# Remainder channels of attention scores and dP: four key chunks at four row positions of TensorE

## The chip, the cores and the metric

The kernel runs on one core of one Trainium2 chip. The metric is the device time of one execution in microseconds; the median of the kernel before is 1481.88 us over three runs (1480.46 to 1482.83).

## The reference

The reference is the forward pass and all gradients of one layer of a Branchformer, for x of shape (2, 4000, 144) in bf16. Only the attention branch bears on this change:

```
xa = layernorm(x)
q, k, v = split(xa @ w_qkv)              # D = 144 each
p = softmax((q @ k.T) * D ** -0.5)       # 4000 x 4000 for each of the two sequences
glob = (p @ v) @ w_att_out
... a local branch (gelu, layernorm, depthwise convolution of 5 taps), merged with glob by
    another convolution of 5 taps and w_merge, added to x
returns out and the gradients of x and of all seven weights
```

There is one head, 144 channels wide. Since 144 = 128 + 16, every product that contracts over channels is split into a part of 128 channels and a remainder of 16.

## The kernel before, in words

The two sequences are worked through one after the other. For each, the 4000 tokens lie as 32 blocks of 125 (NB = 32, PB = 125). The weights are folded ahead of time, so that scores are `Q xa^T` with Q = xa M1 (M1 = scaled w_q w_k^T), and the gradient of the probabilities is `dP = G xa^T` with G the gradient that reaches the attention through the merge convolution, folded with w_v and w_att_out. Both products take the same right-hand side: xa, transposed. It is kept as `xaT_m` (128 channels by 4000 tokens) and, for the other 16 channels, in rows 0 to 15 of `R` (128 by 4000; rows 16 to 111 hold the remainder channels of grad_out, rows 112 to 127 zeros). `pre_pieces` makes these, in four groups of eight blocks: `xat(g)` transposes on TensorE and copies the 16 remainder rows into R on VectorE (L346).

`phase_att` is the stage that the change touches. One step t of its loop (L812) does the following for query block i = t and for the blocks before it, as a software pipeline:

- `jit_mm(t+1)` computes Q and G of the next block into `qb` (two parts of 256 columns, of which 144 are channels and the rest zeros); `jit_tr(t+1)` transposes this into `qt`, four tiles of 128 rows by 125 columns: Q's 128 channels, Q's remainder (16 rows and 112 rows of zeros), and the same two of G.
- `S_pair(t, c2)`, four times: a PSUM tile from the pool `ps_sg` (two tiles of two banks each) takes two key chunks of 500 (CH) tokens. Each chunk is a matmul over 128 channels (L679) and one over the remainder (L680) with all 128 rows of `qt` and `R`, the zeros of `qt` masking the rows of R that don't belong. VectorE then finds the running minimum of the negated scores (L684, L686, one operation of 1000 columns), and ScalarE writes exp(score + that) into `Pbuf` (L687).
- `rescale(t)` brings the first three pairs to the last one's maximum (L692, L696, L698) and starts a DMA transpose of the block's Pbuf into `PT` on SyncE's queue (L699).
- `Y_half(t-1, h)`, two halves: 32 matmuls of PT with xa (L707), and then the row sums' reciprocal, delta, and the scaled copies (L713 to L721).
- `dP_pair(t-1, c2)`, four times: as S_pair with G (L729, L730), and then VectorE writes dS = (dP - delta) * P into `Sbuf`, one operation for each chunk of 500 (L735).
- `Z_half(t-2, h)`: 32 matmuls of the transposed dS (`ST`, by a DMA transpose, L855) with xa (L751); `zt_tr(t-3)` transposes the result.
- `X_group`: dx's share, sixteen blocks in six groups of up to three, each with two or more pairs of matmuls (L790) into a tile of the pool `ps_w` (three banks), added into `acc` by VectorE (L796).
- `local(upto)`: the next few of some 280 small pieces of the local branch, spread over the steps.

PSUM's eight banks are thus taken: four by ps_sg, three by ps_w (X, jit_mm, jit_tr, zt_tr and the local branch), one by Y and Z. An inner loop over s = 0 to 7 (L822) fixes the order: s below 4 has a pair of scores, s from 4 on a pair of dP, and the rest stands between them. The framework orders each engine's queue by this sequence, but lets an instruction that is ready sooner by its own estimate go ahead, except where an edge forbids it. Each engine then works strictly through its queue.

## Time and profile before

The profiled execution took 1482.13 us, its span from the first to the last instruction 1480.4 us, at a mean granted TensorE clock of 0.984.

| stretch of the span, us | what runs there |
|---|---|
| 0 to 52 | loads, layernorm, weights, transposes of the first sequence |
| 52 to 643 | attention and local branch, first sequence (32 steps; the first L684 at 62.0, the last at 638.9) |
| 643 to 772 | merge and gradients, first sequence; preparation of the second |
| 772 to 1358 | attention and local branch, second sequence (L684 from 775.1 to 1351.2) |
| 1358 to 1480 | merge, gradients, weights' gradients |

| group of instructions | count | busy us | mean ns |
|---|---|---|---|
| L679, scores, 128 channels, PE | 512 | 194.1 | 379 |
| L680, scores, remainder, PE | 512 | 193.5 | 378 |
| L729, dP, 128 channels, PE | 512 | 192.8 | 377 |
| L730, dP, remainder, PE | 512 | 191.4 | 374 |
| L735, dS, VectorE | 512 | 355.8 | 731 |
| L687, exponentials, ScalarE | 256 | | 1097 (median) |

How to read it: PE is TensorE's matmuls, PEld its weight loads, DVE VectorE, ACT ScalarE, POOL GpSimd, SP SyncE. The duration of a matmul includes the way through the array, so matmuls one behind the other overlap in the records: their cost in a full queue is the distance from one start to the next, which is less than the mean duration.

### The profile page before, as it was taken

How to read it: one execution, taken by the hardware profiler on the slowest of the kernel's cores; microseconds unless marked ns; L12 is line 12 of the kernel's file. 1: busy time of each engine (PE TensorE's matmuls, PEld its weight loads, DVE VectorE, ACT ScalarE, POOL GpSimd, SP SyncE). 2: the span in 40 equal slices, each digit the busy share in tenths (PEclk: the TensorE clock that was granted, in tenths of full speed). 3: DMA queues.
4: the chain of work that ended last, by engine and by line, in shares of the span. 5: the costliest groups of instructions: out<-in, count | busy, mean ns of one | idle time of the engine just before them, and what ended most of it. 6: DMA issues, size and time to landing. Idle time of an engine off the chain costs nothing. (4 is left out here: it accounts for less than half of the span.)

```text
span 1480.4 us, 39159 instructions
## 1 busy us (share of the span) xinstructions
PE 1387.0 (94%) x16184; PEld 1191.1 (80%) x16184; DVE 1218.0 (82%) x3061; ACT 851.2 (57%) x1538; POOL 282.1 (19%) x493
## 2 busy tenths in 40 slices
PE   2789999999999999997888999999999999999898
PEld 1568888888888888887875888888888888888797
DVE  6689898988898988887638998889898889888754
ACT  1666666666566655632637666666666656554182
POOL 8210111110111110027521112120101010101420
PEclk9899999999999999998999999999999999999999
DMA  3176666666665665577215765667666666666812
GB/s 103 27 145 122 121 121 121 111 126 113 117 116 113 121 121 103 115 136 209 64 54 106 138 122 113 111 118 126 116 123 121 121 120 121 119 115 123 214 35 64
DMA packets 559360, 170.44 MB, mean 115 GB/s; under 512 B 542443, under 2 KB 554093, under 8 KB 559136
## 3 DMA queue, kind: packets, MB, share of 16 engines
q1 hardware_dynamic: 553338, 155.43, 55.6%
q0 software_dynamic: 4768, 12.14, 3.2%
q8 instruction: 126, 2.06, 0.6%
q10 hardware_dynamic: 1076, 0.38, 0.1%
q14 instruction: 52, 0.43, 0.1%
HBM read 21.07 MB, written 14.16 MB: 24 GB/s over the span
## 5 line engine op out<-in xcount | busy, mean ns | idle before, releaser
L735 DVE SCALAR_TENSOR_TENSOR Sbuf<-ps,delta,Pbuf 125x500 bf16<-125x500 f32 x512 | 355.8, 731 | 29.5 <-PE ps L730 26.8
L790 PE MATMUL X<-QBs,Sbuf 125*125 125x144 bf16 x2048 | 302.7, 226 | 6.0 <-DVE acc L796 2.6
L790 PE MATMUL X<-QBs,Pbuf 125*125 125x144 bf16 x2048 | 301.9, 226 | 0.0
L790 PEld LDWEIGHTS <-Pbuf 125*125 125x125 bf16 x2048 | 261.7, 137 | 14.3 <-issue 9.8
L790 PEld LDWEIGHTS <-Sbuf 125*125 125x125 bf16 x2048 | 261.8, 136 | 7.7 <-DVE Sbuf L735 2.0
L796 DVE TENSOR_TENSOR acc<-X,acc 125x432 f32<-125x432 f32 x372 | 203.2, 549 | 32.7 <-PE X L790 31.7
L679 PE MATMUL ps<-xaT_m,qt 128*125 128x500 bf16 x512 | 194.1, 379 | 10.7 <-ACT Pbuf L687 9.5
L729 PE MATMUL ps<-xaT_m,qt 128*125 128x500 bf16 x512 | 192.8, 377 | 6.1 <-ACT Pbuf L687 4.6
L680 PE MATMUL ps<-R,qt 128*125 128x500 bf16 x512 | 193.5, 378 | 0.0
L730 PE MATMUL ps<-R,qt 128*125 128x500 bf16 x512 | 191.4, 374 | 0.0
L707 PEld LDWEIGHTS <-PT 125*125 125x125 bf16 x2048 | 153.5, 138 | 24.2 <-DMA PT<-Pbuf 6.4
L751 PEld LDWEIGHTS <-ST 125*125 125x125 bf16 x1984 | 147.1, 137 | 18.1 <-DMA ST<-Sbuf 0.6
L707 PE MATMUL yz<-xa_aug,PT 125*125 125x145 bf16 x2048 | 157.2, 229 | 3.7 <-DMA PT<-Pbuf 3.6
L751 PE MATMUL yz<-xa_aug,ST 125*125 125x144 bf16 x1984 | 151.0, 227 | 0.4 <-DMA ST<-Sbuf 0.4
L680 PEld LDWEIGHTS <-qt 128*125 128x125 bf16 x512 | 70.3, 137 | 32.6 <-issue 13.3
L543 POOL TENSOR_TENSOR A_dwc<-l_fl,A_dwc 128x512 f32<-128x512 f32 (+2 forms) x48 | 35.9, 748 | 293.8 <-ACT l_fl L542 293.8
L730 PEld LDWEIGHTS <-qt 128*125 128x125 bf16 x512 | 69.5, 136 | 26.1 <-issue 6.7
L684 DVE TENSOR_SCALAR_CACHE_REDUCE Pbuf<-ps 125x1000 bf16<-125x1000 f32 x64 | 76.6, 1197 | 14.6 <-PE ps L680 14.4
L729 PEld LDWEIGHTS <-qt 128*125 128x125 bf16 x512 | 70.0, 137 | 22.5 <-DVE Sbuf L735 2.0
L679 PEld LDWEIGHTS <-qt 128*125 128x125 bf16 x512 | 70.3, 137 | 21.8 <-ACT qt L663 1.2
L755 ACT ACTIVATE zn<-yz,rl 125x144 bf16<-125x144 f32 x64 | 24.3, 379 | 109.7 <-PE yz L751 109.7
L413 POOL TENSOR_SCALAR l_a<-l_sq 125x576 bf16<-125x576 bf16 x32 | 21.5, 672 | 294.5 <-ACT l_sq L411 254.2
(806 smaller groups left out, 3058.6 us busy)
## 6 DMA issues: line engine op xcount, KB each, us to landing
Yn_d<-yn SPq DMA_DIRECT2D x64, 35.2 KB
Zn_d<-zn SPq DMA_DIRECT2D x64, 35.2 KB
ug_d<-ugr SPq DMA_DIRECT2D x32, 70.3 KB
xo<-in_x_dram SPq DMA_DIRECT2D x16, 140.6 KB
out_dram<-dxo SPq DMA_DIRECT2D x16, 140.6 KB
go_h<-in_grad_out_dram POOLq DMA_DIRECT2D x4, 504.0 KB, 7.0
Zn<-Zn_d SPq DMA_DIRECT2D x4, 504.0 KB
PT<-Pbuf SPq DMA_TRANSPOSE x64
```

The lines of the kernel that those rows point to most:

```text
L543: nc.gpsimd.tensor_tensor(acc, fl[0:rows, 0:n], acc, op=ALU.add)
L679: nc.tensor.matmul(ps[:, h, 0:CH], qt[:, 0, :], xaTm[:, cs], start=True, stop=False)
L680: nc.tensor.matmul(ps[:, h, 0:CH], qt[:, 1, :], R[:, cs], start=False, stop=True)
L684: nc.vector.tensor_scalar(pdst, src, -1.0, None, op0=ALU.mult, op1=ALU.min, accum_out=nm[:, 0:1])
L707: nc.tensor.matmul(Y, PT[0:PB, j, 0:PB], xaa[:, j, :], start=(j == 0), stop=(j == NB - 1))
L729: nc.tensor.matmul(ps[:, h, 0:CH], qt[:, 2, :], xaTm[:, cs], start=True, stop=False)
L730: nc.tensor.matmul(ps[:, h, 0:CH], qt[:, 3, :], R[:, cs], start=False, stop=True)
L735: nc.vector.scalar_tensor_tensor(sdst, ps[:, h, 0:CH].rearrange("p (a b) -> p a b", b=PB), DL[i][:], psrc, op0=ALU.subtract, op1=ALU.mult)
L751: nc.tensor.matmul(Z, ST[0:PB, j, 0:PB], xaa[:, j, 0:D], start=(j == 0), stop=(j == NB - 1))
L755: nc.scalar.activation(zn[:, 0:D], Z, ACT.Copy, scale=RL.pop(i)[:])
L790: nc.tensor.matmul(X[:, jj, :], l, r, start=(n_ == 0), stop=(n_ == len(ops) - 1))
L796: nc.vector.tensor_tensor(av, X[:, 0:nj, :], av, op=ALU.add)
```

## The change

Four things are changed, the first three of them together.

1. The 16 remainder channels of xa are laid out a second time, in a new tile `XR` (128 by 2 by 500): key chunk c stands in rows 32 (c mod 4) to 32 (c mod 4) + 15, at place c // 4. Two DMAs on SyncE's queue for each xat(g) copy them there from R. On the other side, GpSimd repeats the 16 remainder columns of qb at columns 32, 64 and 96 of the same 128, so that after jit_tr the remainder tiles of qt hold the 16 rows four times, at rows 0, 32, 64 and 96.
2. `S_pair` and `dP_pair` become `S_quad` and `dP_quad`, two of each a step. A quad takes both tiles of ps_sg, issues the four matmuls over 128 channels, and behind the last of them (an edge, `issue_after`, holds the order) the four remainder matmuls, each with 16 rows at its own row position and into its own PSUM bank.
3. The order of a step is written out anew: scores 0; zt_tr, X, local; jit_mm, X, local; scores 1; both halves of Y; rescale; local, X, local; dP 0; jit_tr, X, local, X; dP 1; both halves of Z; X, local; what is left of X.
4. dS is computed with one VectorE operation of 1000 columns for two chunks, in place of one for each.

```diff
@@ -344,6 +344,9 @@
             for bi in range(8):
                 nc.tensor.transpose(pr[0:DR, bi, 0:PB], S.xa_aug[:, 8 * g + bi, 128:D], W.ident[0:PB, 0:PB])
             nc.vector.tensor_copy(v8(S.R, 8 * g, 8)[0:DR], pr[0:DR, :, 0:PB])
+            for c in (2 * g, 2 * g + 1):
+                r = 32 * (c % 4)
+                nc.sync.dma_start(S.XR[r:r + DR, c // 4, :], S.R[0:DR, c * CH:(c + 1) * CH])
 
         def go_rem():
             nc.gpsimd.tensor_copy(S.go_r[:], go_q[:, :, 128:D])
@@ -637,7 +640,7 @@
             nc.gpsimd.memset(t_[:, :, D:256], 0.0)
         for t_ in znr:
             nc.gpsimd.memset(t_[:, D:256], 0.0)
-        xaTm, R, xaa = S.xaT_m, S.R, S.xa_aug
+        xaTm, R, XR, xaa = S.xaT_m, S.R, S.XR, S.xa_aug
         QT, QB, RL, DL, YZ, ZN, ZT, NM, DHT = {}, {}, {}, {}, {}, {}, {}, {}, {}
         units = local_units(k, W, b, S, A, es_loc, DHT, ps_w)
 
@@ -651,6 +654,8 @@
                 nc.tensor.matmul(pj[:, D:2 * D], S.goT[:, h * PB:(h + 1) * PB], W.VUT[:, kk, 0:D], start=False, stop=(kk == 4))
             qb = qbr[i % 3]
             nc.scalar.copy(qb[:, :, 0:D], pj[:].rearrange("p (a b) -> p a b", b=D))
+            rem_ = qb[:, :, 128:256].rearrange("p a (r c) -> p a r c", c=32)[:, :, :, 0:DR]
+            nc.gpsimd.tensor_copy(rem_[:, :, 1:4, :], rem_[:, :, 0:1, :].to_broadcast([PB, 2, 3, DR]))
             QB[i] = qb
 
         def jit_tr(i):
@@ -666,25 +671,35 @@
         def pchunk(pb, c2):
             return Pbuf[0:PB, pb, c2 * 1024:(c2 + 1) * 1024]
 
-        def S_pair(i, c2):
-            qt = QT[i]
-            if c2 == 0:
+        def quad(qt, q, m):
+
+
+            pp = [ps_sg.tile([PB, 2, 512], F32, tag="sg", name="ps") for _ in range(2)]
+            for r in range(4):
+                c = 4 * m + r
+                mm = nc.tensor.matmul(pp[r // 2][:, r % 2, 0:CH], qt[:, q, :], xaTm[:, c * CH:(c + 1) * CH], start=True, stop=False)
+            with tc.issue_after(mm.ins):
+                for r in range(4):
+                    rs = slice(32 * r, 32 * r + DR)
+                    nc.tensor.matmul(pp[r // 2][:, r % 2, 0:CH], qt[rs, q + 1, :], XR[rs, m, :], start=False, stop=True)
+            return pp
+
+        def v2(ap):
+            return ap.rearrange("p h (a b) -> p h a b", b=PB)
+
+        def S_quad(i, m):
+            if m == 0:
                 nm_ = small.tile([PB, 8], F32, tag="nm")
                 NM[i] = nm_
             nm = NM[i]
-            ps = ps_sg.tile([PB, 2, 512], F32, tag="sg")
-            for h in range(2):
-                c = 2 * c2 + h
-                cs = slice(c * CH, (c + 1) * CH)
-                nc.tensor.matmul(ps[:, h, 0:CH], qt[:, 0, :], xaTm[:, cs], start=True, stop=False)
-                nc.tensor.matmul(ps[:, h, 0:CH], qt[:, 1, :], R[:, cs], start=False, stop=True)
-            src = ps[:, :, 0:CH].rearrange("p h (a b) -> p h a b", b=PB)
-            pdst = pchunk(i % NPB, c2).rearrange("p (h a b) -> p h a b", h=2, b=128)[:, :, :, 0:PB]
-            if c2 == 0:
-                nc.vector.tensor_scalar(pdst, src, -1.0, None, op0=ALU.mult, op1=ALU.min, accum_out=nm[:, 0:1])
-            else:
-                nc.vector.tensor_scalar(pdst, src, -1.0, nm[:, c2 - 1:c2], op0=ALU.mult, op1=ALU.min, accum_out=nm[:, c2:c2 + 1])
-            nc.scalar.activation(pdst, src, ACT.Exp, bias=nm[:, c2:c2 + 1], scale=1.0)
+            for c2, ps in enumerate(quad(QT[i], 0, m), 2 * m):
+                src = v2(ps[:, :, 0:CH])
+                pdst = pchunk(i % NPB, c2).rearrange("p (h a b) -> p h a b", h=2, b=128)[:, :, :, 0:PB]
+                if c2 == 0:
+                    nc.vector.tensor_scalar(pdst, src, -1.0, None, op0=ALU.mult, op1=ALU.min, accum_out=nm[:, 0:1])
+                else:
+                    nc.vector.tensor_scalar(pdst, src, -1.0, nm[:, c2 - 1:c2], op0=ALU.mult, op1=ALU.min, accum_out=nm[:, c2:c2 + 1])
+                nc.scalar.activation(pdst, src, ACT.Exp, bias=nm[:, c2:c2 + 1], scale=1.0)
 
         def rescale(i):
             nm = NM.pop(i)
@@ -720,19 +735,11 @@
             nc.sync.dma_start(S.Yn_d[:, i, :], yn[:])
             nc.scalar.activation(QBs[:, i % NPB], qb[:, :, 0:D], ACT.Copy, scale=rl[:])
 
-        def dP_pair(i, c2):
-            qt = QT[i]
-            ps = ps_sg.tile([PB, 2, 512], F32, tag="sg")
-            for h in range(2):
-                c = 2 * c2 + h
-                cs = slice(c * CH, (c + 1) * CH)
-                nc.tensor.matmul(ps[:, h, 0:CH], qt[:, 2, :], xaTm[:, cs], start=True, stop=False)
-                nc.tensor.matmul(ps[:, h, 0:CH], qt[:, 3, :], R[:, cs], start=False, stop=True)
-            for h in range(2):
-                c = 2 * c2 + h
-                psrc = Pbuf[0:PB, i % NPB, c * 512:(c + 1) * 512].rearrange("p (a b) -> p a b", b=128)[:, :, 0:PB]
-                sdst = Sbuf[0:PB, i % NDB, c * 512:(c + 1) * 512].rearrange("p (a b) -> p a b", b=128)[:, :, 0:PB]
-                nc.vector.scalar_tensor_tensor(sdst, ps[:, h, 0:CH].rearrange("p (a b) -> p a b", b=PB), DL[i][:], psrc, op0=ALU.subtract, op1=ALU.mult)
+        def dP_quad(i, m):
+            for c2, ps in enumerate(quad(QT[i], 2, m), 2 * m):
+                psrc = pchunk(i % NPB, c2).rearrange("p (h a b) -> p h a b", h=2, b=128)[:, :, :, 0:PB]
+                sdst = Sbuf[0:PB, i % NDB, c2 * 1024:(c2 + 1) * 1024].rearrange("p (h a b) -> p h a b", h=2, b=128)[:, :, :, 0:PB]
+                nc.vector.scalar_tensor_tensor(sdst, v2(ps[:, :, 0:CH]), DL[i][:], psrc, op0=ALU.subtract, op1=ALU.mult)
 
         def last_tr(c2):
 
@@ -819,37 +826,44 @@
                 for _ in range(n):
                     if xg:
                         X_group(*xg.pop(0))
-            for s in range(8):
-                if s < 4 and ok(t):
-                    S_pair(t, s)
-                if s >= 4 and ok(t - 1):
-                    dP_pair(t - 1, s - 4)
-                if t == NB and s == 4:
-                    M.late_y()
-                if s == 0:
-                    if ok(t - 3):
-                        zt_tr(t - 3)
-                    x(1)
-                elif s == 1:
-                    if ok(t + 1):
-                        jit_mm(t + 1)
-                    x(1)
-                elif s in (2, 3):
-                    if ok(t - 1):
-                        Y_half(t - 1, s - 2)
-                    if s == 3 and ok(t):
-                        rescale(t)
-                elif s == 4:
-                    if ok(t + 1):
-                        jit_tr(t + 1)
-                    x(1)
-                elif s == 5:
-                    x(1)
-                else:
-                    if ok(t - 2) and t < NB:
-                        Z_half(t - 2, s - 6)
-                    x(1)
-                local(-(-n_units * (8 * t + s + 1) // (8 * (NB - 1))))
+            def loc(f):
+                local(-(-int(n_units * (t + f) * 1000) // (1000 * (NB - 1))))
+            if ok(t):
+                S_quad(t, 0)
+            if ok(t - 3):
+                zt_tr(t - 3)
+            x(1)
+            loc(0.2)
+            if ok(t + 1):
+                jit_mm(t + 1)
+            x(1)
+            loc(0.4)
+            if ok(t):
+                S_quad(t, 1)
+            for h in range(2):
+                if ok(t - 1):
+                    Y_half(t - 1, h)
+            if ok(t):
+                rescale(t)
+            loc(0.5)
+            x(1)
+            loc(0.6)
+            if ok(t - 1):
+                dP_quad(t - 1, 0)
+            if t == NB:
+                M.late_y()
+            if ok(t + 1):
+                jit_tr(t + 1)
+            x(1)
+            loc(0.85)
+            x(1)
+            if ok(t - 1):
+                dP_quad(t - 1, 1)
+            for h in range(2):
+                if ok(t - 2) and t < NB:
+                    Z_half(t - 2, h)
+            x(1)
+            loc(1.0)
             x(6)
             if t < NB and ok(t - 1):
                 nc.sync.dma_start_transpose(out=ST[:], in_=Sbuf[:, (t - 1) % NDB, :])
@@ -1287,6 +1301,7 @@
     bx = pool(ctx, "bx", "left")
     xaT_m = bx.tile([128, T], BF, name="xaT_m")
     R = bx.tile([128, T], BF, name="R")
+    XR = bx.tile([128, 2, CH], BF, name="XR")
     go_r = bx.tile([PB, NB + 6, DR], BF, name="go_r")
     goT = bx.tile([128, (NB + 4) * PB], BF, name="goT")
     acc = bx.tile([PB, NB, D], F32, name="acc")
@@ -1296,7 +1311,7 @@
     SS = [K() for _ in range(B)]
     SS[0].xa_aug = px0.tile([PB, NB, D + 1], BF, name="xa_aug0")
     for b, S in enumerate(SS):
-        S.xaT_m, S.R, S.go_r, S.goT, S.acc, S.rstd_x = xaT_m, R, go_r, goT, acc, rstd[b]
+        S.xaT_m, S.R, S.XR, S.go_r, S.goT, S.acc, S.rstd_x = xaT_m, R, XR, go_r, goT, acc, rstd[b]
         for nm in ("Yn", "ug", "Zn"):
             setattr(S, nm + "_d", tc.dram_tile([PB, NB, D], BF, name="%s_d%d" % (nm, b)))
     A = K()
```

## The prediction

> **What bounds the kernel now.** I read the page first, then busy time by window, then the waits inside the attention stage, then single instructions in order of time.
>
> The page's busy line and the two attention stages (one for each of the two sequences) as windows:
>
> ```profile
> PE 1387.0 (94%) x16184; PEld 1191.1 (80%) x16184; DVE 1218.0 (82%) x3061; ACT 851.2 (57%) x1538; POOL 282.1 (19%) x493
> ```
>
> ```profile
> 74.00:643.00 569.00, 557.61 (x6361) 475.34 (x6361) 501.82 (x1163) 353.09 (x632) 69.01 (x109) 0.99 0.65 120
> 783.00:1358.00 575.00, 561.20 (x6394) 477.36 (x6394) 507.30 (x1174) 359.35 (x642) 81.34 (x136) 1.00 0.66 121
> ```
>
> The columns are window, its length, busy PE, PEld, DVE, ACT, POOL, granted clock, DMA share, GB/s. These stages hold 1144 of the 1480.4 us, and in them PE is busy 1118.8 us (98%), DVE 1009.1 (88%). The granted clock is 1.00. A busy PE alone proves little, so the waits in 111 to 629 us come next (us in total, times, longest):
>
> ```profile
> PE ps L729 <- ACT Pbuf L687: 1.3, 2, 0.8
> ```
>
> ```profile
> DVE Pbuf L686 <- PE ps L680: 23.8, 34, 1.9
> DVE Sbuf L735 <- PE ps L730: 12.2, 20, 1.5
> ```
>
> All waits of PE that this view lists add up to under 8 us in 518; DVE's to about 56, nearly all for PE. So PE's queue sets the pace, and an instruction less on it is worth its issue time as long as DVE can follow. The first scores reduction of a step (L684) comes every 18.9 us in the steady steps (mean of 28 intervals in the timeline); start to start, PE's instructions fill 18.6 us of that and DVE's 16.8.
>
> The prices are start-to-start distances. Timeline of PE, one pair of score groups, and of DVE:
>
> ```profile
> 316.00 0.38 PE L679 MATMUL ps<-xaT_m,qt 128*125 128x500 bf16 x1
> 316.21 0.37 PE L680 MATMUL ps<-R,qt 128*125 128x500 bf16 x1
> 316.42 0.37 PE L679 MATMUL ps<-xaT_m,qt 128*125 128x500 bf16 x1
> 316.63 0.37 PE L680 MATMUL ps<-R,qt 128*125 128x500 bf16 x1
> 316.84 1.22 PE L707 MATMUL yz<-xa_aug,PT 125*125 125x145 bf16 x16
> ```
>
> ```profile
> 306.15 1.38 DVE L735 SCALAR_TENSOR_TENSOR Sbuf<-ps,delta,Pbuf 125x500 bf16<-125x500 f32 x2
> ...
> 315.50 1.25 DVE L686 TENSOR_SCALAR_CACHE_REDUCE Pbuf<-ps,nm__4761 125x1000 bf16<-125x1000 f32 x1
> 316.68 0.08 DVE L686 DVE_READ_ACCUMULATOR Pbuf<-ps,nm__4761 125x1 f32 x1
> ```
>
> A matmul of 500 columns costs 0.21 us of PE whether its 128 rows hold 128 channels (L679) or 16 (L680). Two L735 of 500 columns take 1.38, one 0.73, so the second adds 0.65; one operation of 1000 columns (L686) lets the next start after 1.18.
>
> **The change, part by part.**
>
> **Remainder matmuls.** L680 and L730 are 512 each, 1024 in all, or 256 groups of four. Removed per group: 4 x 0.21 = 0.84 us. Added per group: four matmuls of 16 rows at four row positions, and two passages, from full-height to 16-row matmuls and back. No row has four matmuls at different row positions, so their time is bounded: 0.21 if they run at once, 0.84 if in turn. Between: each needs its own weight load, and X's pairs of load and matmul (L790) start every 0.063 us, so loads one behind the other put the fourth matmul 3 x 0.063 = 0.19 after the first, and the group takes 0.19 + 0.21 = 0.40. I take 0.40, because that is the nearest row on loads. The passage has a row: full-height and 16-row transposes in turn, in the preparation of the weights.
>
> ```profile
> 42.47 0.26 PE L231 MATMUL pt<-ident,Wi 128*96 128x128 bf16 x1
> 42.65 0.20 PE L232 MATMUL pt<-ident,Wi 16*96 16x16 bf16 x1
> 42.79 0.26 PE L231 MATMUL pt<-ident,Wi 128*96 128x128 bf16 x1
> 42.97 0.20 PE L232 MATMUL pt<-ident,Wi 16*96 16x16 bf16 x1
> ```
>
> A pair takes 42.79 - 42.47 = 0.32 us. Eight transposes of one height (L341 at 48.85) take 0.60 with the last one's 0.22, so they start 0.055 apart and two would take 0.11; the passage there and back costs 0.32 - 0.11 = 0.21. So a group costs 0.40 + 0.21 = 0.61 in place of 0.84: 0.23 saved, 256 x 0.23 = **-59 us**. Bounds: 0.21 + 0.21 gives -108 us, 0.84 + 0.21 gives +54 us.
>
> The Trainium skill, "TensorE: Matmul & The Clock Gate", section Part 3 (Packing small matmuls), gives a speedup of 3.07 for four 32-row tiles at 512 columns; no run here shows it yet. By it the group would take 0.84 / 3.07 = 0.27 (an estimate from that page), the saving be 0.36 a group or 92 us, and the sum below come to about 1409 us.
>
> **PSUM hand-over.** The pool for scores and dP has two tiles of two chunks. Before, a pair takes one tile and PE can be one pair ahead. Now a group of four chunks takes both, and its third main matmul waits until the group before has been read out of the second tile. From the last issue of a group: 0.21 until DVE starts (316.84 to 317.05), then for scores two reductions of 1.2 and the exponential of the second (L687, 1.1, starting 0.1 later): 3.8. For dP: 0.21 + 2 x 1.18 + 0.06 until PE follows (L735's end to L729 at 303.68) = 2.6. PE's own work in the meantime, from the same timeline (X group of 12: 0.75; Y or Z: 2.1; jit_mm 0.50; jit_tr 0.22; zt_tr 0.11; the local units 2.4 a step in the new shares), with 0.42 for the two main matmuls in the first tile:
> - scores 0 to scores 1: 0.11 + 1.50 + 0.50 + 0.96 + 0.42 = 3.5 against 3.8: 0.3 short
> - scores 1 to dP 0: 2.1 + 0.75 + 0.48 + 0.42 = 3.75 against 3.8: even
> - dP 0 to dP 1: 0.22 + 1.50 + 0.60 + 0.42 = 2.7 against 2.6: covered
> - dP 1 to the next step: 2.1 + 0.75 + 0.36 + 0.42 = 3.6 against 2.6: covered
>
> That is 0.3 a step if DVE takes each group at once: 64 x 0.3 = **+19 us**. It doesn't always do so now: in the timeline of steps 2 to 29, L684/L686 start 0.23 us later than the 0.04 behind their matmul that is the least, L735 0.66 later. With these on top the first two and the third hand-over are short by 0.53, 0.26 and 0.52: 1.3 a step, +84 us. Below 19 it goes to 0 if X or local matmuls stand in the gap. I take 19, since DVE gets free time in this change and catches up whenever PE waits.
>
> **dS in operations of 1000 columns.** Four pairs a step at 1.18 in place of 0.73 + 0.65 - 0.08 = 1.30: 0.12 x 4 = 0.5 us a step, 31 us of DVE over 64 steps. DVE isn't the bound, so **0** in the sum. It takes DVE to 16.3 of a step. If nothing were saved there, 16.8 would still lie below PE's new 17.7 (18.6 - 4 x 0.23).
>
> **The rest.** The POOL copy that repeats the 16 channels three times: nearest rows are L455 (125x64, 0.24) and L433 (125x288, 0.42), so some 0.35, 64 times, on an engine busy 59.7 of 518 us. It lies between the copy of qb (ends 314.56) and the transposes of qb (318.78): 4.2 us of slack, so 0; without cover 22 us. Behind it on POOL stand the local units' copies and sums, which it delays by 0.35. The sixteen copies into XR go on SP's queue: the nearest issue is L460 (0.65), and landings of POOL's DMAs lie between 2.1 and 10.3 us. The last copy of R ends at 50.7 and 763.5, the first score matmul starts at 59.9 and about 772, so they have 9 us: 0, at most 2 us. SP waits there for L346; behind it stand stores of finished output (L1052, every 4.6 us), which nothing waits for. The order of Y, Z, X and local units is new, their count is not: 0. X's sums (L796) now find DVE taken for 2.4 us by a group in place of 1.2; three buffers cover that (PE waited 1.3 us in 518 for them), taken as 0, and up to 1.2 us a step or 77 us if the cover is gone.
>
> **Sum.** 1482.13 us is the profiled execution (span 1480.4; the median of three is 1481.88): 1482.1 - 59 + 19 = **1442 us**, and the 0.25 us between the two don't move it.
>
> **The rivals.**
> 1. *The hand-over eats the gain.* At each group PE stands at the third main matmul because DVE, in its own order, is still at sums and local work. For it: at most pairs DVE now starts late (by 0.66 at dP). Against: DVE waited 56 us for PE in 518, so the lateness is PE's order, not want of DVE time. It decides from 0.92 us of waits a step (4 x 0.23); at today's lateness it is 1.3: 1482 - 59 + 84 = **1507 us**, slower. The Trainium skill, "TensorEngine Tiling (Array Packing)", section PSUM Bottleneck, warns of the same: tiling speeds up TensorE, not the reading out of PSUM.
> 2. *The four don't overlap*, and the change doesn't do what it says: 1482 + 54 + 19 = **1555 us**. For it: nothing in this trace ever overlaps two matmuls. Against: nothing either; only the rows' heights allow it.
> 3. *They run wholly at once*, loads hidden: 1482 - 108 + 19 = **1393 us**. For it: weight loads in this trace lie under matmuls that run. Against: after a passage, L232's load starts only 0.15 us after L231 began, so the first load isn't hidden. The skill's 3.07 above lies between this and my forecast.
> 4. *Waits and saving cancel*: 1470 to 1494.
>
> **How the numbers follow.** Forecast (1415 to 1470) 0.40; rival 1 0.25; rival 2 0.07; rival 3 0.20; rival 4 0.08, of which 0.03 within 0.2% (about what a measurement here can tell from no change), 0.02 faster, 0.03 slower. Faster 0.40 + 0.20 + 0.02 = 0.62, same 0.03, slower 0.25 + 0.07 + 0.03 = 0.35. The range runs from just below rival 3 to past rival 1 with part of X's 77 us: 1385 to 1530; it leaves out rival 2 and the tails.
>
> **What would show it.** The four remainder matmuls of a group should start some 0.06 apart (near 0: rival 3; 0.21: rival 2); the next full-height matmul should start 0.6 after the fourth main one ended its issue. PE's waits for Pbuf (L687's successor) and Sbuf in a steady stage should rise from 2 to about 8 us; 25 or more is rival 1. dS should show 256 operations near 1.25 us. The step should go from 18.9 to 18.3. The prediction fails if the four start 0.21 apart, or if PE's idle time a step passes 0.9 us.

## The result and the profile after

The changed kernel takes 1535.17 us (median; 1532.82 to 1537.37) against 1481.17 (1477.91 to 1482.83) for the kernel before on the same chip: a ratio of 1.0359, interval 1.0345 to 1.0374. It is 54 us slower. The forecast was 1442 us, the range 1385 to 1530; the time lies past the range, on the side of rival 1.

The lines have moved: main matmuls L680, remainders L684 (scores and dP alike), reductions L699 and L701, exponentials L702, rescale L711, Y L722, dS L742, X L797, sums L803. First the busy line of the page, then three windows: the two attention stages and the steady stretch 111 to 629 us (window, length, busy PE, PEld, DVE, ACT, POOL, granted clock, DMA share, GB/s).

```profile
PE 1339.5 (87%) x16184; PEld 1086.5 (71%) x16184; DVE 1193.8 (78%) x2805; ACT 851.0 (55%) x1538; POOL 301.8 (20%) x557
```

```profile
74.00:660.00 586.00, 533.72 (x6351) 425.23 (x6351) 489.28 (x1040) 351.93 (x629) 76.27 (x134) 0.99 0.55 116
800.00:1406.00 606.00, 541.72 (x6410) 430.70 (x6410) 497.71 (x1058) 359.93 (x639) 89.90 (x164) 0.98 0.63 115
111.00:629.00 518.00, 473.60 (x5703) 379.26 (x5701) 433.72 (x924) 315.99 (x567) 68.04 (x119) 1.00 0.54 114
```

PE is busy 1075 of 1192 us in the two stages (90%, before 98%), and no other engine has come up: DVE falls to 83%, ACT stays near 60%. No engine is full now. Where the time went is in the waits of 111 to 629 us (total us, times, longest) and in the chain that ended last (share of the span by engine):

```profile
PE ps L680 <- ACT Pbuf L702: 22.9, 44, 1.3
...
DVE Pbuf L701 <- PE ps L684: 13.3, 16, 1.6
DVE Pbuf L699 <- PE ps L684: 11.4, 13, 1.8
...
PE ps L680 <- DVE Sbuf L742: 8.6, 21, 0.9
```

```profile
DVE 35%; PE 33%; ACT 15%; DMA 6%; issue 6%; POOL 5%; DVEq 0%; POOLq 0%; SPq 0%; ACTq 0%
```

PE's main matmuls wait 31.5 us for the readers of their PSUM tiles, where this stretch showed 1.8 us of such waits before, and under 8 us of PE's waits in all. At the same time DVE still waits 24.7 us for PE's scores (29.9 before). Each waits for the other: DVE has 35, PE 33 and ACT 15% of the chain.

The groups (line, engine, operation, out and in, count; busy us, mean ns of one; idle time ahead and what ended most of it):

```profile
L680 PE MATMUL ps<-xaT_m,qt 128*125 128x500 bf16 x1024 | 298.4, 381 | 97.8 <-ACT Pbuf L702 64.9
L742 DVE SCALAR_TENSOR_TENSOR Sbuf<-ps,delta,Pbuf 125x1000 bf16<-125x1000 f32 x256 | 311.0, 1253 | 16.4 <-PE ps L684 16.3
...
L684 PE MATMUL ps<-XR,qt 16*125 16x500 bf16 x1024 | 112.9, 428 | 0.0
...
L684 PEld LDWEIGHTS <-qt 16*125 16x125 bf16 x1024 | 35.9, 129 | 98.4 <-issue 98.4
```

The remainders do overlap: 1024 of 428 ns would be 438 us one behind the other, and the union is 112.9, a quarter. Their weight loads overlap as well: 1024 x 129 ns = 132, the union 35.9. One hand-over, from the second scores group of a step to the first of dP, on three engines, as timelines of PE, DVE and ACT (start, duration, engine, line, operation; in brackets the idle time before it and what ended it):

```profile
306.32 0.43 PE L684 MATMUL ps<-XR,qt 16*125 16x500 bf16 x4
...
309.88 0.58 PE L680 MATMUL ps<-xaT_m,qt 128*125 128x500 bf16 x2
311.44 0.58 PE L680 MATMUL ps<-xaT_m,qt 128*125 128x500 bf16 x2 [0.97 <-ACT Pbuf L702]
311.95 0.43 PE L684 MATMUL ps<-XR,qt 16*125 16x500 bf16 x4
312.31 0.39 PE L666 MATMUL pt<-ident,qb 125*128 125x125 bf16 x4
```

```profile
306.95 0.46 DVE L419 TENSOR_TENSOR l_z<-l_a,l_hs 125x576 bf16<-125x576 bf16 x1 [0.34 <-POOL l_a L416]
307.33 1.25 DVE L701 TENSOR_SCALAR_CACHE_REDUCE Pbuf<-ps,nm__4433 125x1000 bf16<-125x1000 f32 x1
308.51 0.08 DVE L701 DVE_READ_ACCUMULATOR Pbuf<-ps,nm__4433 125x1 f32 x1
308.71 1.26 DVE L701 TENSOR_SCALAR_CACHE_REDUCE Pbuf<-ps,nm__4433 125x1000 bf16<-125x1000 f32 x1
...
313.30 2.42 DVE L742 SCALAR_TENSOR_TENSOR Sbuf<-ps,delta,Pbuf 125x1000 bf16<-125x1000 f32 x2
```

```profile
308.75 1.08 ACT L702 ACTIVATE Pbuf<-ps,nm__4433 125x1000 bf16<-125x1000 f32 x1
309.73 0.67 ACT L467 ACTIVATE l_th<-l_q 125x576 bf16<-125x576 bf16 x1
310.30 1.09 ACT L702 ACTIVATE Pbuf<-ps,nm__4433 125x1000 bf16<-125x1000 f32 x1
```

The scores' group ends at 306.75. DVE waits 0.34 us for POOL and does a local operation first, so the reduction starts at 307.33, 0.58 late. The second one, which takes the first one's minimum, follows 1.38 later, and the second exponential stands behind a local one on ACT (L467) and ends at 311.39. Only then, at 311.44, may PE write the next group's second tile: the first two mains, begun at 309.88, ended at 310.46, and PE stood 0.97 us. The group then ends at 312.38, and dS starts at 313.30, late again by 0.92, behind the rescale. What is late on one engine is handed to the next, because neither side has a tile to go on with.

In steps: the interval from one step's first reduction to the next was 18.90 us in both sequences; it is 19.45 in the first and 19.69 in the second. Of the 54.4 us of span, 19.6 lie between the first steps' and the last steps' first reductions in the first sequence, 28.5 in the second, 7.3 behind the last of them, and the first comes 1.1 earlier. Start to start, PE's instructions filled 18.61 us of a step before. The granted clock doesn't explain it: in 111 to 629 us it shows 1.00 for both kernels, and the steps of the first sequence are 0.55 us longer all the same.

### The profile page after: what moved, and what is told of

It reads as the page before. It is cut to its first block, busy times and chain, and to the rows that moved or that the text cites. A ratio compares the mean times of both kernels' runs of the same rounds, so it can differ in the third digit from the quotient of the medians.

```text
span 1534.8 us, 39000 instructions
## 1 busy us (share of the span) xinstructions
PE 1339.5 (87%) x16184; PEld 1086.5 (71%) x16184; DVE 1193.8 (78%) x2805; ACT 851.0 (55%) x1538; POOL 301.8 (20%) x557
## 4 chain that ended last, share of the span: by engine, by line
DVE 35%; PE 33%; ACT 15%; DMA 6%; issue 6%; POOL 5%; DVEq 0%; POOLq 0%; SPq 0%; ACTq 0%
DVE Pbuf L701 10%; DVE Sbuf L742 8%; PE ps L680 7%; ACT Pbuf L702 6%; PE X L797 5%; PE yz L758 5%; DVE Pbuf L699 4%; PE ps L684 3%; DMA PT<-Pbuf 3%; DVE acc L803 3%; PE po L1062 2%; DVE Pbuf L711 2%; PE yz L722 2%; ACT QBs L736 1%; PE Hps L983 1%
## 5 line engine op out<-in xcount | busy, mean ns | idle before, releaser
L680 PE MATMUL ps<-xaT_m,qt 128*125 128x500 bf16 x1024 | 298.4, 381 | 97.8 <-ACT Pbuf L702 64.9
L742 DVE SCALAR_TENSOR_TENSOR Sbuf<-ps,delta,Pbuf 125x1000 bf16<-125x1000 f32 x256 | 311.0, 1253 | 16.4 <-PE ps L684 16.3
L797 PE MATMUL X<-QBs,Sbuf 125*125 125x144 bf16 x2048 | 305.3, 227 | 12.3 <-ACT qt L668 2.2
L797 PE MATMUL X<-QBs,Pbuf 125*125 125x144 bf16 x2048 | 303.4, 226 | 0.0
L797 PEld LDWEIGHTS <-Pbuf 125*125 125x125 bf16 x2048 | 262.2, 137 | 21.3 <-issue 18.2
L797 PEld LDWEIGHTS <-Sbuf 125*125 125x125 bf16 x2048 | 262.6, 137 | 8.5 <-issue 6.3
L803 DVE TENSOR_TENSOR acc<-X,acc 125x432 f32<-125x432 f32 x372 | 201.4, 550 | 57.1 <-PE X L797 55.8
L680 PEld LDWEIGHTS <-qt 128*125 128x125 bf16 x1024 | 129.0, 138 | 135.2 <-issue 116.6
L722 PE MATMUL yz<-xa_aug,PT 125*125 125x145 bf16 x2048 | 163.6, 234 | 9.6 <-DMA PT<-Pbuf 9.6
L722 PEld LDWEIGHTS <-PT 125*125 125x125 bf16 x2048 | 149.6, 141 | 29.5 <-issue 13.5
L684 PE MATMUL ps<-XR,qt 16*125 16x500 bf16 x1024 | 112.9, 428 | 0.0
L699 DVE TENSOR_SCALAR_CACHE_REDUCE Pbuf<-ps 125x1000 bf16<-125x1000 f32 x64 | 76.7, 1198 | 37.9 <-PE ps L684 37.8
L684 PEld LDWEIGHTS <-qt 16*125 16x125 bf16 x1024 | 35.9, 129 | 98.4 <-issue 98.4
L711 DVE TENSOR_SCALAR Pbuf<-Pbuf,f 125x1000 bf16<-125x1000 bf16 x128 | 57.5, 493 | 41.0 <-ACT f L707 40.5
L713 ACT ACTIVATE Pbuf<-Pbuf,f 125x1000 bf16<-125x1000 bf16 x64 | 72.8, 1138 | 0.5
L658 POOL COPY qb<-qb 125x96 bf16<-125x96 bf16 x64 | 19.1, 298 | 242.6 <-ACT qb L656 242.1
L523 ACT ACTIVATE l_w<-gd,c,nc 125x144 f32<-125x144 bf16 x64 | 29.2, 501 | 49.7 <-DVE nc L519 49.7
```

Of the source, the lines that this page charges most:

```text
L680: mm = nc.tensor.matmul(pp[r // 2][:, r % 2, 0:CH], qt[:, q, :], xaTm[:, c * CH:(c + 1) * CH], start=True, stop=False)
L684: nc.tensor.matmul(pp[r // 2][:, r % 2, 0:CH], qt[rs, q + 1, :], XR[rs, m, :], start=False, stop=True)
L699: nc.vector.tensor_scalar(pdst, src, -1.0, None, op0=ALU.mult, op1=ALU.min, accum_out=nm[:, 0:1])
L711: nc.vector.tensor_scalar(pdst, pdst, f[:, c2:c2 + 1], None, op0=ALU.mult)
L713: nc.scalar.activation(pdst, pdst, ACT.Copy, scale=f[:, c2:c2 + 1])
L722: nc.tensor.matmul(Y, PT[0:PB, j, 0:PB], xaa[:, j, :], start=(j == 0), stop=(j == NB - 1))
```

## The experiments

All ratios are to the kernel before, timed on the same chip (its medians there: 1480.9 to 1482.9 us). The step is the mean of 28 steps, as in the prediction.

| run | us | ratio, interval | step in the first, second sequence, us |
|---|---|---|---|
| the change | 1535.2 | 1.0359, 1.0345 to 1.0374 | 19.45, 19.69 |
| quad_full_height | 1549.6 | 1.0459, 1.0435 to 1.0484 | 19.74, 19.95 |
| new_order_by_tile | 1496.5 | 1.0110, 1.0080 to 1.0139 | 19.26, 19.25 |
| before_ds1000 | 1478.7 | 0.9973, 0.9958 to 0.9987 | 18.83, 18.83 |
| quad_exp_from_sbuf | 1510.0 | 1.0193, 1.0167 to 1.0219 | 19.24, 19.30 |
| before_exp_from_sbuf | 1482.1 | 0.9999, 0.9984 to 1.0014 | 18.89, 19.00 |
| quad_alternating | 1652.9 | 1.1151, 1.1116 to 1.1187 | 20.64, 21.83 |
| pairs_two_positions | 1500.7 | 1.0114, 1.0086 to 1.0143 | 19.12, 19.19 |
| copies_only | 1474.8 | 0.9952, 0.9937 to 0.9967 | 18.83, 18.83 |
| mixed_groups | 1536.0 | 1.0371, 1.0341 to 1.0402 | 19.17, 19.56 |
| old_order_dp_quads | 1501.5 | 1.0121, 1.0094 to 1.0148 | 19.12, 19.16 |
| old_order_scores_quads | 1532.7 | 1.0332, 1.0303 to 1.0361 | 19.44, 19.64 |
| old_order_quads | 1541.2 | 1.0394, 1.0369 to 1.0419 | 19.56, 19.71 |

### The change taken apart

**quad_full_height**: the groups of four with both tiles and the new order stay, but the remainders are again full-height matmuls over R, without XR and GpSimd's copy.

```diff
-                    rs = slice(32 * r, 32 * r + DR)
-                    nc.tensor.matmul(pp[r // 2][:, r % 2, 0:CH], qt[rs, q + 1, :], XR[rs, m, :], start=False, stop=True)
+                    c = 4 * m + r
+                    nc.tensor.matmul(pp[r // 2][:, r % 2, 0:CH], qt[:, q + 1, :], R[:, c * CH:(c + 1) * CH], start=False, stop=True)
```

> The changed kernel with one part undone: the remainder matmuls are again full-height (128 rows of qt and R, 0.21 us each), still four behind four main ones, in the new order and with both PSUM tiles taken by a group. Theory A (the hand-over of both tiles makes PE wait): the row positions themselves save, by the changed kernel's trace, 0.39 us a group, 256 groups, 100 us; the waits between groups depend on the work between them, which stays, so most of the 100 comes on top: 1590 to 1640 us. Rival B (the row positions bring their own loss, through the passage between heights): not slower than the changed kernel, 1480 to 1535.

**new_order_by_tile**: as quad_full_height, but each tile is taken, filled and read by itself.

```diff
-            pp = [ps_sg.tile([PB, 2, 512], F32, tag="sg", name="ps") for _ in range(2)]
...
+            for u in range(2):
+                ps = ps_sg.tile([PB, 2, 512], F32, tag="sg", name="ps")
...
+                    nc.tensor.matmul(ps[:, h, 0:CH], qt[:, q, :], xaTm[:, cs], start=True, stop=False)
+                    nc.tensor.matmul(ps[:, h, 0:CH], qt[:, q + 1, :], R[:, cs], start=False, stop=True)
+                yield ps
```

> The new order of a step, dS in 1000 columns, but full-height remainders issued tile by tile as before (two main and two remainder matmuls complete one tile, and only then the next tile is needed). Theory A (hand-over): with the first tile handed on 0.8 us sooner and PE needing one tile at a time, waits are at most 1 us a step: 18.6 + 1.0 against 18.9, so 1490 to 1530. Rival C (the new order of Y, Z, X and local work is what makes PE wait, whatever the tiles do): the 2.5 us of waits a step that the changed kernel has stay, 18.6 + 2.5 = 21.1, some 140 us over the kernel before: 1600 or more.

**before_ds1000**: the kernel before with dS in operations of 1000 columns, nothing else.

```diff
-            for h in range(2):
...
-                nc.vector.scalar_tensor_tensor(sdst, ps[:, h, 0:CH].rearrange("p (a b) -> p a b", b=PB), DL[i][:], psrc, op0=ALU.subtract, op1=ALU.mult)
+            nc.vector.scalar_tensor_tensor(sdst, ps[:, :, 0:CH].rearrange("p h (a b) -> p h a b", b=PB), DL[i][:], psrc, op0=ALU.subtract, op1=ALU.mult)
```

> The kernel before with one part of the change alone: dS in operations of 1000 columns. Prediction's step: 0.5 us a step of VectorE saved and none of it on the path: 1476 to 1486. Rival D (the longer operation holds VectorE's queue and so delays what PE waits for): 1500 or more.

The last two came out as their first theory had it (1490 to 1530, 1476 to 1486). The kernels form a row in which each differs from the next by one thing: before 1481.8, dS in one operation 1478.7 (-3), the new order tile by tile 1496.5 (+18), the groups that take both tiles 1549.6 (+53), row positions 1535.2 (-14). The range for quad_full_height was missed by both expectations (1590 to 1640, 1480 to 1535): I had taken it that the 100 us of PE time saved by row positions would show in full once they were undone, and they show as 14. In the waits of quad_full_height in the steady stretch, where PE has 0.39 us more to do at each group:

```profile
PE ps L675 <- ACT Pbuf L697: 9.5, 28, 0.9
...
PE ps L675 <- DVE Sbuf L737: 1.6, 5, 0.5
```

These 11 us are 31.5 in the changed kernel. PE is done sooner and stands longer: most of what row positions save turns into waiting for the same readers. Tile by tile, in new_order_by_tile, the same waits are 3.8 us:

```profile
PE ps L675 <- DVE Sbuf L734: 2.6, 10, 0.7
...
PE ps L675 <- ACT Pbuf L694: 1.2, 6, 0.4
```

The largest single term of the loss in this row is the taking of both tiles by one group, +53 us, with the same number of instructions on every engine. Two things go together in it: PE needs both tiles before it can go on, and the first tile of a group is complete later, behind the mains of the second. The runs don't part them. The sizes also hold for this row alone; another way from one kernel to the other, below, gives other ones.

### Does the time for which a tile is held decide?

**quad_exp_from_sbuf** and **before_exp_from_sbuf**: the exponential reads the clipped, negated scores out of Pbuf in SBUF, so that a PSUM tile is free after DVE's reduction, some 1.1 us sooner. The same edit, in the changed kernel and in the kernel before.

```diff
-                nc.scalar.activation(pdst, src, ACT.Exp, bias=nm[:, c2:c2 + 1], scale=1.0)
+                nc.scalar.activation(pdst, pdst, ACT.Exp, bias=nm[:, c2:c2 + 1], scale=-1.0)
```

> The changed kernel, but the exponential takes what the reduction wrote into Pbuf (bf16) in place of the PSUM tile, so a scores tile is free 1.1 us sooner; what it computes is the exponential of the scores clipped by the running maximum, not the softmax, and the number and size of operations stay. Theory A: PE's waits for the exponential (64.9 us listed before L680, and the tails hidden beside them) go, 1440 to 1480 us. Rival C (order of the step): PE waits somewhere else, 1520 to 1540.

> The kernel before with the exponential taken from Pbuf as in quad_exp_from_sbuf (the same clipped scores, not the softmax). Theory A: PE waited 1.3 us for it in 518, so the earlier freeing of a tile is worth nothing here: 1475 to 1487. If the exponential's source alone changes the time (another cost on ScalarE), it shows here: below 1470 or over 1490.

In the kernel before it is worth nothing (0.9999, as expected), in the changed one 25 us, between the two theories' ranges. So with one tile in hand the exponential's time on the tile is covered, and with both tiles taken it isn't. But 25 us isn't the 54: the changed kernel's waits of PE in the same stretch become

```profile
PE ps L680 <- DVE Sbuf L742: 8.4, 15, 1.1
PE X L797 <- ACT qt L668: 6.9, 9, 1.1
PE ps L680 <- DVE Pbuf L701: 4.4, 10, 0.7
```

ACT is gone from the waits of L680, which fall from 31.5 to 13.1 us. But PE's waits in all don't fall (42.1 us, in the changed kernel 41.3): PE now stands elsewhere, most for ACT's copies, as in the second line. The exponential on the tile is thus part of the loss, and what is behind it shows up once it is gone.

**mixed_groups**: each group takes one pair of scores of block t and one of dP of block t - 2, so that a group has one exponential in place of two and four equal turns a step. For this, Pbuf has five blocks, qt four buffers, three buffers of the local branch are made smaller, the second sequence's x is loaded later, the rest of the step is put in another order and the loop has one step more.

```diff
+        def mixed(t, k4):
+            parts, outs = [], []
+            if ok(t):
+                parts.append((QT[t], 0, k4))
+                outs.append((S_out, t, k4))
+            if ok(t - 2):
+                parts.append((QT[t - 2], 2, k4 ^ 1))
+                outs.append((dS_out, t - 2, k4 ^ 1))
+            if parts:
+                for (f, i, c2), ps in zip(outs, group(parts)):
+                    f(i, c2, ps)
```

> Groups of four made of one pair of scores of block t and one pair of dP of block t - 2 (a step later than before, so that delta is always there), at four row positions, four groups a step as in the change. Each group still takes both PSUM tiles, but holds them for one reduction, one dS operation and an exponential beside the latter, some 2.5 us, in place of 3.8 for two pairs of scores. To make room, two scratch tiles of the local branch are bf16, one ring is shorter, and the second sequence's x is loaded later. Theory A (how long a group holds both tiles, added up over the ring): four groups take 4 x (1.2 + 2.5) = 14.8 us a step at least, below PE's own 17.1, so the step is 17.5 to 18.3 in place of 19.5, and with the extra step at each end 1420 to 1470. Rival E (PE and VectorE take turns at each group, however long it holds the tiles): 1500 or more.

My sum over holding times gave 1420 to 1470 and is wrong: it takes as long as the changed kernel. Its waits in the steady stretch:

```profile
PE ps L681 <- ACT Pbuf L704: 21.6, 39, 1.3
...
DVE Pbuf L703 <- PE ps L687: 31.3, 32, 3.6
```

PE waits for the readers, and DVE for PE, as in the changed kernel. The sum had two faults. It took 2.5 us for a group, and in the trace the first tile, with the exponential, is free 2.8 to 3.2 us after the group's issue on average. And it compared totals of a step, where PE stands group by group: 0.9 us a step at the groups' first main matmuls, nothing at the third ones. The steady step is in fact 0.28 and 0.13 us shorter than in the changed kernel; the added step and the longer ends (149.7 us behind the last reduction with which a step begins, against 136.5) take that back. So the run prices neither the holding nor the turn alone.

**quad_alternating**: the changed kernel with the groups in the order scores 0, dP 0, scores 1, dP 1, so that no two groups with exponentials follow each other; rescale, jit_mm and jit_tr move along.

```diff
-            if ok(t):
-                S_quad(t, 1)
             for h in range(2):
                 if ok(t - 1):
                     Y_half(t - 1, h)
...
             if ok(t - 1):
                 dP_quad(t - 1, 0)
...
+            if ok(t):
+                S_quad(t, 1)
```

> The changed kernel with its four groups of a step in another order: scores 0, dP 0, scores 1, dP 1, with Y behind scores 0 and Z behind scores 1, so that the long occupation of the tiles (scores: two reductions and an exponential, 3.8 us) always has the most other PE work behind it (3.5 to 3.9 us with the first two main matmuls of the next group) and the short one (dP, 2.6 us) the least. Theory A (occupation of both tiles against PE work in the gap): shorter than the changed kernel by 20 to 60 us, 1475 to 1515. Rival E (it is not these gaps but the strict turn-taking of PE and VectorE at each group, whatever stands between): 1525 to 1550.

```profile
PE yz L722 <- DMA PT<-Pbuf: 20.4, 14, 2.5
...
PE ps L680 <- ACT Pbuf L702: 10.0, 21, 1.4
...
PE ps L680 <- DVE Sbuf L742: 7.2, 18, 1.1
```

L680's waits do fall, from 31.5 to 17.2 us, but the run is lost to another wait: Y now comes soon after the rescale, and PE stands for the DMA transpose of Pbuf. The granted clock is lower too, 0.97 and 0.95 in the two stages against 0.99 and 0.98. The run tells nothing of the holding times; the order was a bad choice of mine.

### Row positions by themselves

**pairs_two_positions**: the order of the kernel before, one tile at a time; the two remainders of a pair at two row positions behind the two mains; dS in one operation, XR and GpSimd's copy as in the change.

```diff
-                nc.tensor.matmul(ps[:, h, 0:CH], qt[:, 0, :], xaTm[:, cs], start=True, stop=False)
-                nc.tensor.matmul(ps[:, h, 0:CH], qt[:, 1, :], R[:, cs], start=False, stop=True)
+                mm = nc.tensor.matmul(ps[:, h, 0:CH], qt[:, 0, :], xaTm[:, cs], start=True, stop=False)
+            with tc.issue_after(mm.ins):
+                for h in range(2):
+                    c = 2 * c2 + h
+                    rs = slice(32 * (c % 4), 32 * (c % 4) + DR)
+                    nc.tensor.matmul(ps[:, h, 0:CH], qt[rs, 1, :], XR[rs, c // 4, :], start=False, stop=True)
```

> The kernel before in its own order, with pairs (one PSUM tile a time), dS in 1000 columns, and the remainders of a pair at two row positions (XR and the POOL copy as in the change). By the changed kernel's trace a passage and two matmuls at once take 0.30 + 0.35 us behind the last main matmul's start in place of 0.63: 0.02 more a pair, 512 pairs, +10 us: 1480 to 1495. Theory A says no more than that, since one tile stays in hand. Rival B (row positions, XR or the POOL copy cost by themselves): 1510 or more.

1500.7 is just past the first theory's 1480 to 1495 and short of the other's 1510: 22 us slower than before_ds1000, with PE full (window 111 to 629 us):

```profile
111.00:629.00 518.00, 514.45 (x5834) 384.52 (x5831) 442.28 (x942) 320.42 (x576) 67.35 (x120) 1.00 0.56 117
```

No wait has been added, and the passage accounts for nearly all of it. The first remainder starts 0.30 us after the last main, and the next full-height matmul 0.35 after that, so a pair takes 0.21 + 0.65 = 0.86 us in place of 4 x 0.21 = 0.84: some 10 us for 512 pairs. Sixteen matmuls of Y behind it take 1.26 in place of 1.22, and Z's are as much longer: another 10. At two positions nothing is left of the gain.

**copies_only**: the kernel before with the copies into XR, GpSimd's copy and dS in one operation, but remainders over R.

> The kernel before with dS in 1000 columns and, of the row positions, the copies alone: XR is written by its DMAs and the POOL copy repeats qb's remainder columns, but the remainder matmuls are full-height with R as before (R's other rows then enter the scores, so the numbers differ, the work doesn't). Prediction's step: both copies are hidden: 1474 to 1484, as before_ds1000. Then the 22 us of pairs_two_positions over before_ds1000 are the passages'. Rival F: the copies cost (POOL beside VectorE, or qb's chain): 1490 or more, and the passages the rest.

Copies and DMAs cost nothing that can be measured: 1474.8 us, no more than before_ds1000's 1478.7.

### Which groups, and in which order

Three runs in the order of the kernel before: **old_order_dp_quads** has groups of four at row positions for dP alone, **old_order_scores_quads** for scores alone, **old_order_quads** for both (its loop, against the kernel before):

```diff
-                if s < 4 and ok(t):
-                    S_pair(t, s)
-                if s >= 4 and ok(t - 1):
-                    dP_pair(t - 1, s - 4)
+                if s in (0, 2) and ok(t):
+                    S_quad(t, s // 2)
+                if s in (4, 6) and ok(t - 1):
+                    dP_quad(t - 1, s // 2 - 2)
```

> The order of the kernel before; scores in full-height pairs, tile by tile; dP alone in groups of four at four row positions (128 groups in place of 256), dS in operations of 1000 columns, the copies into XR, GpSimd's copy for G's half alone. Theory A (a group that takes both PSUM tiles costs its turn at any place): measured so far, +53 us for 256 groups and -14 for their row positions, +39 together or +0.15 a group; 1478.7 (order before, 1000 columns) + 128 x 0.15 = 1498, range 1488 to 1508. Rival H (only the time a tile is held decides): the two dP groups hold their tiles 2.45 us after their third main matmul, and PE has 2.7 and more of other work behind each, so only the first one's wait for the exponential of the last scores pair is left, 0.25 to 0.5 us x 64 = 16 to 32, against 128 x 0.39 = 50 us of PE saved: 1445 to 1462, faster than both kernels.

> The mirror of the run with dP in groups: the order of the kernel before, scores in groups of four at four row positions, dP in full-height pairs, dS in operations of 1000 columns. Theory A: the same 1498, range 1488 to 1508. Rival H: scores hold their tiles 3.85 us, PE has 2.1 to 3.5 of work behind them, so each of the 128 groups waits some 0.4 to 0.8 us where 0.39 is saved: 1480 to 1530, and at least 25 us more than the run with dP in groups.

> All four groups of the change, in the order of the kernel before (a group in place of the first of each two pairs, nothing in place of the second). If the order's own +18 us (measured tile by tile) and the groups' cost add up, as theory A has it: 1535 - 18 = 1517, range 1508 to 1526. If the new order was the better one for groups of four (rival O: it puts PE's other work between the groups more evenly): 1535 to 1560. Rival H: the sum of its two shares, about 1478.7 + (-25 + 25) = 1480, range 1465 to 1505.

Against 1478.7 us, groups for dP cost 23 us, for scores 54, for both 62. Rival H is out as priced: its dP groups should have been faster than both kernels, and they are slower. But its holding times were too short. Behind a group's third main matmul the second tile is free after 4.1 and 3.7 us for the two dP groups in the trace, not 2.45, and after 5.2 and 5.0 for scores, not 3.85; so the runs refute its price and not that the holding decides. Theory A's equal price at any place holds only for dP (1501.5 in 1488 to 1508); a scores group costs more than twice as much, as H's longer holding has it (31 us between the two runs, at least 25 forecast), and the two don't add up. The waits of the dP run in the steady stretch, where L680 is dP alone and L710 the exponential:

```profile
PE ps L680 <- ACT Pbuf L710: 11.8, 27, 1.5
...
PE ps L680 <- DVE Sbuf L750: 6.6, 16, 0.9
```

Most of it is the first dP group waiting for the last scores pair's exponential, but the second waits too, for dS, which was forecast to be covered. And the two orders: with groups, the order before takes 1541.2 us and the new one 1535.2. So the +18 us of the new order, measured tile by tile, can't be added to the price of the groups: on this way the groups with their row positions cost 62 us, and the order then takes 6 off, where the row above had +18, +53 and -14. With groups of four the new order is no worse; the intervals of the two runs overlap a little (1.0369 to 1.0419 and 1.0345 to 1.0374), so that it is better isn't quite shown.

No version with groups of four is as fast as the kernel before; the nearest is old_order_dp_quads, 1.2% slower. The one version that beats both with the same result is before_ds1000, by 0.27% (0.9973, 0.9958 to 0.9987); copies_only, which has its dS and other scores, lies at 0.9952.

## Why the prediction was wrong

- **What bounds the kernel** was read rightly for the kernel before: PE's queue was full. That an instruction less on it is worth its issue time "as long as DVE can follow" is where it went on to fail, since the change itself took away what let DVE follow.
- **Remainder matmuls, -59 us**: the mechanism holds, and the term was put too low. The four start within 0.01 us of each other, as rival 3 had it, not 0.06 apart: their loads overlap too (35.9 us of union for 132). From the last main's start to the next full-height matmul it is 0.66 us in place of 1.05: 0.39 saved a group, 256 x 0.39 = 100 us by these distances. The passage costs 0.66 - 0.21 - 0.21 = 0.24, forecast 0.21. The Trainium skill's speedup of 3.07 for four row tiles ("TensorE: Matmul & The Clock Gate", section Part 3) gave 0.36 saved with the same passage; the trace has 0.39, close to it. By that step alone the kernel would have come to some 1382 us.
- **PSUM hand-over, +19 us**: this is the step that failed. The hand-over is where the forecast said, but the time for which a group holds its second tile was mis-sized: 3.8 us for scores and 2.6 for dP, from the end of the group's issue, with DVE ready at once. In the trace of 111 to 629 and 850 to 1350 us it is 4.5 and 4.3 us on average for the two scores groups and 3.4 and 2.9 for the two dP groups. Against the prediction's own terms for PE's work (3.5, 3.75, 2.7 and 3.6) the first three are short by 1.0, 0.5 and 0.7, and the fourth is covered: 2.2 us a step in place of 0.3, some 141 us (an estimate from these means).
  - The whole step says the same. PE's own work in it is now 18.61 - 4 x 0.39 = 17.05 us, an estimate, and the step is 19.57 on average: 2.52 us a step in which PE stands or its last matmul's tail runs out, where it was 18.90 - 18.61 = 0.29. That is (2.52 - 0.29) x 64 = about +143 us, the remainder of the step and no measurement of its own. Even the bound of +84 was too low.
  - What made the holding longer: DVE's lateness is 0.29 and 0.19 us at the two scores groups, 0.70 and 0.18 at the two dP groups, much as before (0.23 and 0.66). So it didn't grow, but it isn't so either that DVE "catches up whenever PE waits", although it is idle 3.1 us a step (2.1 before). The rest is in the scores' chain: the second reduction starts 1.4 us behind the first, whose result it takes, not 1.2, and in the first group the second exponential starts 0.2 us behind its reduction, not 0.1. The bound of +84 had the lateness and not these.
  - The sum looked at the third main matmul of a group alone. Of the 1.26 us a step for which PE is recorded as idle ahead of a group's mains, 0.72 stand at the first one, for the first tile. That the estimate comes so near to the 143 is thus in part luck.
  - Rival 1 named this mechanism and the sign. Its 1507 lies nearer to the result than it should: with the 100 us that were really saved it would have been 1466.
- The two sums: -100 from the matmuls, +143 from the hand-over, +11 at the ends (7 behind the last step's first reduction, the rest in the first and last steps): +54.
- **The Trainium skill's section PSUM Bottleneck** ("TensorEngine Tiling (Array Packing)") agrees with the outcome: reading out of PSUM isn't sped up with TensorE, and PE's waits for the readers are 31.5 us in 518. But neither reader is full here (DVE 83%, ACT 60%); it is the time that a group waits and is read that costs, not the readers' sum of work.
- **dS in operations of 1000 columns, 0**: right. 1253 ns each, and -3 us alone (0.9973), the one part that makes the kernel before faster.
- **POOL's copy and XR, 0**: right (copies_only).
- **The new order, 0**: wrong for single tiles (+18 us), about right in what the change does, since with groups of four the older order is no better (1541.2).
- **X's sums, 0**: right; PE's matmuls of X wait 0.2 us for them in the steady stretch.
- **What would show it**: the sign given for rival 1 (25 us or more of PE's waits for Pbuf and Sbuf in the steady stretch) stands at 31.5, and the point at which the prediction fails (0.9 us of idle PE a step) is passed at 1.69 recorded.

The cause is shown as far as this: groups that take both tiles lose the time (+53 us in one order, +62 with row positions in the other), a shorter hold of the tile wins 25 us back and is worth nothing where one tile is taken at a time, and the holding times in the trace give the size. What stays open: how the loss divides between DVE's own order, ACT's own order (L467 ahead of the second exponential), the later first tile and the taking of both tiles itself, and why PE's waits move elsewhere when the exponential leaves the tile. A third tile for scores and dP would have parted them; with all eight banks taken, it wasn't tried.

## What to carry to other kernels

Before matmuls are packed into a larger unit, count the buffers that a unit takes at once: where it takes all of them, the engine that writes and those that read work in turn, and each unit costs the time from the end of its issue until its buffers are free, less the writer's other work in between. Take that time from the readers' queues: how late they start now, which operation needs the result of the one before, and what stands between. Their idle time doesn't mean that they will be ready when a unit arrives. Undo the parts one at a time, and in more than one order: here the matmuls gained some 100 us of PE time as designed, and all of it was lost where the engines meet.

## What the runs showed of the hardware

- Four matmuls of 16 rows at four row positions, into four PSUM banks, run wholly at once: starts within 0.01 us, 0.43 us for all four where one takes 0.428. Their weight loads overlap in the same way.
- The passage between full-height matmuls and these has a price on each side: 0.30 us from the last main's start to the first remainder's (0.21 between full-height ones) and 0.35 from there to the next full-height one. With four remainders it leaves 0.39 us a group, with two nothing.
- The second sequence's steps are longer than the first's in the versions with groups of four (21.83 against 20.64 in quad_alternating, at a granted clock of 0.95 against 0.97); in the changed kernel 19.69 against 19.45, at a granted clock of 0.98 against 0.99; before, both were 18.9, at 0.99 and 1.00. How much of the difference is the clock, the runs don't part.
